# Linear attention and a gated feed-forward on one core: batch 0's first products from two terms, denominators ahead of numerators, wider dummy matmuls, and half a denominator chain moved into layer 2

## The chip, the core and the metric

The kernel runs on one core of a Trainium2 chip. The metric is the device time of one execution in microseconds (us). The engines are TensorE (PE, with its weight loads as PEld), VectorE (DVE), ScalarE (ACT), GpSimd (POOL) and SyncE (SP). The program's tiles live in SBUF, and PE writes its results to eight PSUM banks, which the kernel uses as four pairs.

## The reference

For 8 batches of 8 heads, 576 positions and head width 64, a linear attention; then a feed-forward over the 4608 positions, with 512 inputs, 1536 hidden units and 512 outputs:

```python
phi = lambda x: np.where(x > 0, x, np.exp(x) - 1.0) + 1.0
q_p, k_p = phi(q), phi(k)
kv  = np.einsum('bhsd,bhse->bhde', k_p, v)
z   = np.sum(k_p, axis=2)
num = np.einsum('bhsd,bhde->bhse', q_p, kv)
den = np.einsum('bhsd,bhd->bhs', q_p, z)[..., None] + 1e-06
x   = (num / den).transpose(0, 2, 1, 3).reshape(4608, 512)
g   = x @ w_gate
out = (g * (1 / (1 + np.exp(-g))) * (x @ w_val)) @ w_out
```

In the kernel phi(x) is max(x, 0) + min(exp(x), 1), so it has two terms that are made apart.

## The kernel before

**Layout.** The heads of a batch are handled as two halves, `lp` = 0 and 1, of four heads each. `kp` holds max(k, 0) after `mx_k`, `ek` holds exp(k) after `exp_k` (ACT) and min(exp(k), 1) after `mn_k`; `add_k` adds `ek` into `kp`, which is phi(k). `kv_corner(b, lp, t, first, last)` accumulates 36 small matmuls (64x64) of k's part `t` with v into the pair `kvp[b]`; `r_copy` copies the result to `R`. `zt` sums k's part over positions by matmuls with two columns, and `zr_copy` spreads that sum into `Zr`.

**Groups.** The positions are cut into nine groups `g` of 512. In each, layer 1 goes over 12 blocks `fb` of 128 hidden units: `l1(g, fb)` issues four matmuls with `w_gate` and four with `w_val` (128x512 each) into a pair; ACT makes `sil`, and DVE the product `hT`. Layer 2 (`lay2`, `l2_mm`) then goes over four tiles `t` of 128 positions, 12 matmuls each, and `l2_out` copies the tile out, on ACT for even `t` and on DVE for odd `t`, and stores it.

**Order.** The order is written out by hand (`manual_schedule`): each engine executes its instructions in the order of the program text, and waits only for what they need. The list `sl[fb]` holds what is issued behind `l1(g, fb)`. The pairs go round in a ring: `pair()` takes the one that was used longest ago, so a matmul that writes it waits until its last reader is through.

**The start (batch 0, lines 424 to 461).** q is transposed on PE (`qtr`), and `ph[lp]` makes phi of it: an exponential on ACT, a min on DVE, and a max-and-add on DVE. For `lp` = 1 that last operation is cut in two, `t_add_half`. `t_corners(0, Zr, lp, ps)` are the den matmuls of a half, `lnrd` their reciprocal on ACT (a logarithm and an exponential), `t_corners(0, R, lp, ps)` the num matmuls, and `x_t` multiplies num by the reciprocal into `xT` on DVE. `warm(n)` issues `n` dummy matmuls of 128 columns, whose results nobody reads; `WARM` holds their numbers. The first chunks of layer 1 (`l1_mm`, L273) are interleaved with this, and the loop over `fb` (`l1`, L289) follows.

**Batch 2 and later.** Batch 2's q is handled during group 1: `zsum` (DVE) sums phi(k), `zb` (one matmul and an ACT copy into `zbc`) spreads the sum, and the chain

```python
at: s3_prod(b, 0)          at+3: s3_prod(b, 1)
at+1: s3_reduce, s3_recip  at+4: s3_reduce, s3_recip
at+2: s3_scale, dtr        at+5: s3_scale, dtr
```

multiplies, sums, takes the reciprocal, scales `qp`, and transposes it by a DMA (`dtr`, issued by SP) into `qT`. In group 1 `at` is 6, so the last entries are behind the blocks 10 and 11. Ahead of layer 2's last tile `block(g)` issues `num` and `x_copy` for group g + 1. Between layer 1 and layer 2, POOL copies one element of `qT` into `gate` (L640), the place that the second `dtr` writes last, and only then issues the loads of batch g + 3 (L101).

Of the kernel before, what the change touches and what calls it, by code (L numbers as in the profile page):

```python
# [13 lines left out]
P = 128  # L14
# [3 lines left out]
def kernel(  # L18
# [10 lines left out]
    nc = tc.nc  # L29
# [10 lines left out]
    EPS = 1e-6  # L40
    SC = 4096.0
    NB = 3
    WARM = (36, 10, 20, 8, 6)

    sb = ctx.enter_context(tc.tile_pool(name="sb", bufs=1))
    pp = ctx.enter_context(tc.tile_pool(name="ps", bufs=1, space=bass.MemoryType.PSUM))
# [2 lines left out]
    def many(shape, dt, name, n=2):  # L49
        return [sb.tile(shape, dt, name=f"{name}_{i}") for i in range(n)]  # L50
# [4 lines left out]
    ek = many([P, 2, J, 2 * D], FP16, "ek")  # L55
    eq = many([P, HL, J * D], FP16, "eq")
    kp = many([P, 2, J, 2 * D], FP16, "kp")
# [4 lines left out]
    Zr = many([P, 2, 2, D], FP16, "Zr")  # L62
# [17 lines left out]
    ones = sb.tile([P, P], FP16, name="ones")  # L80
# [7 lines left out]
    pp4 = [[pp.tile([P, 512], FP32, name=f"pp_{2 * i + e}") for e in range(2)] for i in range(4)]  # L88
# [15 lines left out]
    def ld2(src, dst, b):  # L104
        ld(src, dst, b, 0)
        ld(src, dst, b, 1)
# [10 lines left out]
    def act(out, in_, func=AF.Copy, scale=1.0, bias=0.0):  # L117
        nc.scalar.activation(out=out, in_=in_, func=func, bias=bias, scale=scale)  # L118

    def warm(n):  # L120
        for _ in range(n):
            nc.tensor.matmul(out=pp4[2][1][:, 0:P], lhsT=ones[:, :], rhs=ones[:, :], start=True, stop=True)

    def hs(lp):
        return slice(2 * lp, 2 * lp + 2)
# [1 line left out]
    def jl(t, b, lp):  # L127
        return t[b % 2][:, lp, :, :].rearrange("p j (l d) -> p l j d", d=D)

    def lj(t, b, lp):  # L130
        return t[b % NB][:, hs(lp), :].rearrange("p l (j d) -> p l j d", d=D)
# [7 lines left out]
    def mx_k(b, lp):  # L139
        nc.vector.tensor_scalar(out=jl(kp, b, lp), in0=lj(kr, b, lp), scalar1=0.0, scalar2=None, op0=ALU.max)  # L140
# [13 lines left out]
    def add_k(b, lp):  # L154
        a = kp[b % 2][:, lp, :, :]
        nc.vector.tensor_tensor(out=a, in0=ek[b % 2][:, lp, :, :], in1=a, op=ALU.add)  # L156
# [19 lines left out]
    def kv_corner(b, lp, t, first, last):  # L176
        ps = kvp[b]
        for j in range(J):
            for l2 in range(2):
                for hh in range(2):  # L180
                    rows = slice(C * hh, C * hh + C)
                    nc.tensor.matmul(out=ps[hh][D * l2:D * l2 + D, D * lp:D * lp + D],  # L182
                                     lhsT=t[b % 2][rows, lp, j, D * l2:D * l2 + D],
                                     rhs=vr[b % NB][rows, 2 * lp + l2, D * j:D * j + D],
                                     start=(first and j == 0), stop=(last and j == J - 1))
# [6 lines left out]
    def r_copy(b, l0, l1, engs):  # L192
        for hh in range(2):
            src = kvp[b][hh][:, D * l0:D * l1].rearrange("p (l d) -> p l d", d=D)
            if engs[hh] == "A":
                act(R[b % 3][:, l0:l1, hh, :], src)
            else:
                nc.vector.tensor_copy(out=R[b % 3][:, l0:l1, hh, :], in_=src)
# [38 lines left out]
    def units(g):  # L237
        us = [(u // J, u % J) for u in range(U * g, U * g + U)]
        res = []
        for b in sorted(set(u[0] for u in us)):  # L240
            js = [j for (bb, j) in us if bb == b]
            res.append((b, js[0], js[-1] + 1, C * us.index((b, js[0]))))
        return us, res
# [146 lines left out]
    def zt(b, lp, ps, t, first, last):  # L390
        for j in range(J):
            nc.tensor.matmul(out=ps[:, 0:2], lhsT=t[b % 2][:, lp, j, :], rhs=ob[:, 0:P:C],
                             start=(first and j == 0), stop=(last and j == J - 1))
# [5 lines left out]
    def lnrd(ps, i, w0=0, w1=512):  # L399
        for l2 in range(2):  # L400
            act(lnt[2 * i + l2][:, w0:w1], ps[l2][:, w0:w1], AF.Ln, bias=epsb[:, 0:1])
            act(rd[i][:, l2, w0:w1], lnt[2 * i + l2][:, w0:w1], AF.Exp, scale=-1.0)
# [8 lines left out]
    def t_corners(g, W, lp, ps):  # L411
        for (b, j0, j1, c0) in units(g)[1]:
            corners(ps, W[b], b, lp, j0, j1, c0)

    def t_add_half(lp, ps, h):
        a = qT[0][:, lp, 4 * h:4 * h + 4, :, :].rearrange("p j h c -> p (j h c)")
        nc.vector.scalar_tensor_tensor(out=a, in0=ps[:, 256 * h:256 * h + 256].bitcast(FP16), scalar=0.0, in1=a,
                                       op0=ALU.max, op1=ALU.add)

    pq = pp4[0]  # L420
    kvp[0] = pp4[1]
    ph = [t_phi_main(0, lp, pq[lp]) for lp in range(2)]
    for l in range(2):
        nc.vector.tensor_copy(out=qr[0][:, l, :], in_=q32[:, l, :])
    warm(WARM[0])
    for lp in range(2):
        qtr(0, lp, pq[lp])
        warm(WARM[1 + lp])
        ph[lp][0]()
# [3 lines left out]
    ph[0][2]()  # L433
    mx_k(0, 0)
    zt(0, 0, pp4[3][0], kp, True, False)
    warm(WARM[3])
    mn_k(0, 0)
    zt(0, 0, pp4[3][0], ek, False, True)
    ph[1][1]()
    zr_copy(0, 0, pp4[3][0])  # L440
    warm(WARM[4])
    t_corners(0, Zr, 0, pp4[2])
    lnrd(pp4[2], 0)
    mx_k(0, 1)
    mn_k(0, 1)
    zt(0, 1, pp4[3][1], kp, True, False)
    zt(0, 1, pp4[3][1], ek, False, True)
    add_k(0, 0)
    kv_corner(0, 0, kp, True, True)
    zr_copy(0, 1, pp4[3][1])  # L450
    t_add_half(1, pq[1], 0)
    r_copy(0, 0, 1, "VV")
    t_add_half(1, pq[1], 1)
    t_corners(0, R, 0, pp4[0])
    x_t(0, 0, pp4[0], (0,))
    t_corners(0, Zr, 1, pp4[3])
    lnrd(pp4[3], 1)
    kv_corner(0, 1, kp, True, False)
    kv_corner(0, 1, ek, False, True)
    x_t(0, 0, pp4[0], (1,))  # L460
# [14 lines left out]
    def none():  # L475
        return [[] for _ in range(FB)], [[] for _ in range(4)]

    def lam(f, *a):
        return lambda: f(*a)
# [26 lines left out]
    def chain(b, at):  # L506
        return {
            at: [lam(s3_prod, b, 0)],
            at + 1: [lam(s3_reduce, b, 0), lam(s3_recip, b, 0)],
            at + 2: [lam(s3_scale, b, 0), lam(dtr, b, 0)],  # L510
            at + 3: [lam(s3_prod, b, 1)],
            at + 4: [lam(s3_reduce, b, 1), lam(s3_recip, b, 1)],
            at + 5: [lam(s3_scale, b, 1), lam(dtr, b, 1)],
        }
# [93 lines left out]
    for g in range(NG):  # L608
        b1, b2 = g + 1, g + 2
        if g == 0:  # L610
            sl = period0()
        else:
            sl, _ = none()
            if g == 1:
                sl[1] = [lam(zsum, b1)]
                sl[4] = [lam(phi_q, b1, 0), lam(zb, b1)]
                sl[5] = [lam(phi_q, b1, 1)]
                ch = chain(b1, 6)
            elif b1 < B:
                sl[0] = [lam(phi_q, b1, 0)]  # L620
                sl[1] = [lam(phi_q, b1, 1)]
                ch = chain(b1, 2)
            else:
                ch = {}
            for f, v_ in ch.items():
                sl[min(f, FB - 1)] += v_
        for fb in range(FB):
            if g == 0:
                if fb < 2:
                    continue  # L630
                if fb == 4:
                    ld2(k, kr, 2)
                    ld2(q, qr, 2)
                    ld2(v, vr, 2)
            l1(g, fb)
            for f in sl[fb]:
                f()
        if g + 3 < B:
            if g > 0:
                nc.gpsimd.tensor_copy(out=gate[:, :], in_=qT[b1 % 2][:, 1, J - 1, 1, C - 1:C])  # L640
            ld2(k, kr, g + 3)
            ld2(v, vr, g + 3)
            if g > 0:
                ld2(q, qr, g + 3)
        if g == 0:
            layer2_0()
            ld2(q, qr, 3)
        else:
            for t in range(4):
                if t == 0 and b2 < B:  # L650
                    exp_k(b2, 0)
                    exp_k(b2, 1)
                    exp_q(b2, 0)
                    exp_q(b2, 1)
                    phi_k(b2, 0)
                    phi_k(b2, 1)
                    zsum(b2)
                if g == 1 and t == 2:
                    kv_all(b1)
                    r_copy(b1, 0, 2, "AA")  # L660
                if t == 3:
                    block(g)
                if g == NG - 1 and t == 3:
                    l2_open(g, t)
                    o = None
                    for (n0, n1) in ((0, 256), (256, 512)):
                        for fb in range(FB):
                            l2_mm(g, t, fb, n0, n1)
                        o = l2_out(g, t, "V" if n0 == 0 else "A", n0, n1, o)
                    continue  # L670
                lay2(g, t)
                l2_out(g, t, "AV"[t % 2])
            if b2 < B:
                zb(b2)
# [30 lines left out]
```

## Time and profile before

| | |
|---|---|
| median of 5 runs | 320.27 us (319.1 to 320.51) |
| profiled execution | 320.51 us; its span in the trace 318.6 us |
| granted TensorE clock, mean | 0.987 |
| PE busy | 310.7 us, 98% of the span |
| PEld busy | 148.1 us, 46% |
| DVE busy | 203.6 us, 64% |
| ACT busy | 150.8 us, 47% |
| POOL busy | 48.6 us, 15% |
| moved by DMA | 32.52 MB in 41163 packets |

Times in the profile are counted from the span's start. The time of an execution is longer than the span, by 1.9 us here. "Granted clock" is the share of the full TensorE clock. In a timeline row the first number is the start, the second the duration; what ended the engine's idle time stands in brackets. Matmuls are pipelined: the spacing of their starts is their cost, and the duration printed includes a tail that the next one overlaps.

### The profile page before, as it was taken

To read this page: it belongs to the slowest core of one execution; us is meant where nothing else is said; L and a number is where in the kernel's file an instruction comes from. 1 tells how busy PE (TensorE), PEld (TensorE's weight loads), DVE (VectorE), ACT (ScalarE), POOL (GpSimd) and SP (SyncE) were. 2 spreads that over 40 slices of the span, in tenths; PEclk is the share of its full clock that TensorE was granted. 3 is DMA by queue.
4 is the path that set the end of the run, shared out by engine and by line. 5 is a ranking of instruction groups with operands and counts; after the bars stand their busy time and mean duration, and the time that the engine had idled before them with its cause. 6 is when DMAs were issued, how large, how long until landed. Compare 5 with 4: busy or idle time off the path is not lost.

```text
span 318.6 us, 5702 instructions
## 1 busy us (share of the span) xinstructions
PE 310.7 (98%) x2276; PEld 148.1 (46%) x2276; DVE 203.6 (64%) x356; ACT 150.8 (47%) x227; POOL 48.6 (15%) x73
## 2 busy tenths in 40 slices
PE   7899999999999999999999999999999999999994
PEld 6644444444544454444444454445444444444443
DVE  2844885999849874987499739973992343234420
ACT  2764859736543474347533753385331333133311
POOL 7665343000400050005000600000000000000000
PEclk9879999999999999999999999999999999999999
DMA  8999999911694389037903790215023400140014
GB/s 155 197 198 199 206 206 207 248 46 37 113 209 75 74 116 237 5 74 110 246 3 66 106 239 21 50 29 130 0 39 70 99 3 1 33 101 0 0 33 101
DMA packets 41163, 32.52 MB, mean 102 GB/s; under 512 B 16432, under 2 KB 36400, under 8 KB 41136
## 3 DMA queue, kind: packets, MB, share of 16 engines
q0 software_dynamic: 20736, 18.58, 38.0%
q1 hardware_dynamic: 20320, 13.51, 17.3%
q8 instruction: 18, 0.29, 0.4%
q10 hardware_dynamic: 80, 0.07, 0.1%
q14 instruction: 9, 0.07, 0.1%
HBM read 37.75 MB, written 9.44 MB: 148 GB/s over the span
## 4 chain that ended last, share of the span: by engine, by line
PE 87%; ACT 5%; DVE 4%; DMA 2%; issue 1%; POOLq 0%
PE pp L289 54%; PE pp L296 27%; DMA qr<-in_q_dram 2%; PE pp L251 2%; PE pp L182 2%; PE pp L273 2%; ACT lnt L118 1%; DVE hT L282 1%; ACT ek L118 1%; ACT rd L118 1%; ACT eq L118 1%; PE pp L367 1%; ACT L118 0%; DVE den L217 0%; DVE qp L226 0%
## 5 line engine op out<-in xcount | busy, mean ns | idle before, releaser
L118 ACT ACTIVATE sil<-pp 128x512 f16<-128x512 f32 x108 | 63.3, 597 | 103.1 <-PE pp L289 90.6
L289 PE MATMUL pp<-xT,wg 128*128 128x512 f16 x424 | 108.8, 379 | 0.0
L289 PE MATMUL pp<-xT,wv 128*128 128x512 f16 x424 | 108.8, 379 | 0.0
L282 DVE SCALAR_TENSOR_TENSOR hT<-pp,sil 128x512 f16<-128x512 f32 x108 | 72.0, 680 | 48.1 <-PE pp L289 34.5
L296 PE MATMUL pp<-wo,hT 128*128 128x512 f16 (+1 forms) x444 | 97.7, 374 | 0.9 <-DVE osb L319 0.5
L296 PEld LDWEIGHTS <-hT 128*128 128x128 f16 x444 | 42.0, 98 | 49.4 <-issue 1.9
L289 PEld LDWEIGHTS <-wv 128*128 128x128 f16 x424 | 41.5, 98 | 50.0
L289 PEld LDWEIGHTS <-wg 128*128 128x128 f16 x424 | 41.5, 98 | 49.3
L319 DVE TENSOR_SCALAR osb<-pp 128x512 f32<-128x512 f32 (+1 forms) x20 | 13.2, 674 | 31.4 <-PE pp L296 31.4
L118 ACT ACTIVATE osb<-pp 128x512 f32<-128x512 f32 (+1 forms) x17 | 9.8, 579 | 34.9 <-PE pp L296 34.9
L118 ACT ACT_TABLE_LOAD x14 | 18.0, 1283 | 2.8 <-PE pp L289 2.6
L640 POOL COPY gate<-qT 128x1 f16<-128x1 f16 x4 | 1.5, 379 | 107.4 <-DVE hT L282 77.1
L118 ACT ACTIVATE ek<-kr 128x1152 f16<-128x1152 f16 x16 | 17.8, 1154 | 0.2
L226 DVE TENSOR_TENSOR qp<-qp,rden 128x1152 f16<-128x1152 f16 x12 | 16.1, 1346 | 0.0
L217 DVE TENSOR_REDUCE den<-prod 128x18 f32<-128x1152 f16 x12 | 16.1, 1342 | 0.0
L268 DVE TENSOR_SCALAR xT<-pp 128x512 f16<-128x512 f32 (+1 forms) x14 | 8.7, 667 | 7.4 <-PE pp L251 7.3
L118 ACT ACTIVATE eq<-qr 128x1152 f16<-128x1152 f16 x12 | 13.2, 1148 | 0.0
L101 POOL DMA_DIRECT2D vr<-in_v_dram x16 | 11.8, 736 | 5.2 <-DMA wo<-in_moe_w_out_dram 1.8
L101 POOL DMA_DIRECT2D kr<-in_k_dram x16 | 11.6, 724 | 5.6 <-DMA wo<-in_moe_w_out_dram 1.9
L101 POOL DMA_DIRECT2D qr<-in_q_dram x15 | 10.8, 723 | 6.5 <-DMA qr<-in_q_dram 1.9
L156 DVE TENSOR_TENSOR kp<-ek,kp 128x1152 f16<-128x1152 f16 x15 | 11.4, 758 | 0.5
L144 DVE TENSOR_SCALAR ek<-ek 128x1152 f16<-128x1152 f16 x16 | 7.3, 456 | 6.0 <-ACT ek L118 6.0
(67 smaller groups left out, 182.5 us busy)
## 6 DMA issues: line engine op xcount, KB each, us to landing
out_dram<-osb SPq DMA_DIRECT2D x70, 128.0 KB, 5.0
kr<-in_k_dram POOLq DMA_DIRECT2D x16, 288.0 KB, 6.9
vr<-in_v_dram POOLq DMA_DIRECT2D x16, 288.0 KB, 10.2
qr<-in_q_dram POOLq DMA_DIRECT2D x15, 288.0 KB, 12.2
wo<-in_moe_w_out_dram POOLq DMA_DIRECT2D x3, 512.0 KB, 13.5
wg<-in_moe_w_gate_dram POOLq DMA_DIRECT2D x5, 256.0 KB, 9.3
wv<-in_moe_w_val_dram POOLq DMA_DIRECT2D x5, 256.0 KB, 9.8
q<-in_q_dram SPq DMA_DIRECT2D x1, 576.0 KB, 3.7
```

Source lines behind the costliest of these rows:

```text
L101: nc.gpsimd.dma_start(out=dst[b % NB][:, 2 * lp:2 * lp + 2, :], in_=src[b].rearrange("(l a) (c j) d -> (a c) l (j d)", a=2, j=J)[:, 2 * lp ...
L118: nc.scalar.activation(out=out, in_=in_, func=func, bias=bias, scale=scale)
L144: nc.vector.tensor_scalar(out=a, in0=a, scalar1=1.0, scalar2=None, op0=ALU.min)
L156: nc.vector.tensor_tensor(out=a, in0=ek[b % 2][:, lp, :, :], in1=a, op=ALU.add)
L182: nc.tensor.matmul(out=ps[hh][D * l2:D * l2 + D, D * lp:D * lp + D], lhsT=t[b % 2][rows, lp, j, D * l2:D * l2 + D], rhs=vr[b % NB][rows, 2 ...
L217: nc.vector.tensor_reduce(out=den[:, c, :], in_=prod[:, :, :].rearrange("p j (l d) -> p (j l) d", d=D), axis=AX.X, op=ALU.add)
L226: nc.vector.tensor_tensor(out=qv, in0=qv, in1=rden[:, c, :].unsqueeze(2).to_broadcast([P, 2 * J, D]), op=ALU.mult)
L268: nc.vector.tensor_scalar(out=dst, in0=ps[l2][:, c0:], scalar1=1.0 / SC, scalar2=None, op0=ALU.mult)
L282: nc.vector.scalar_tensor_tensor(out=hT[g % 2][:, fb, :], in0=ps[1][:, :], scalar=SC, in1=s[:, :], op0=ALU.mult, op1=ALU.mult)
L289: nc.tensor.matmul(out=ps[h][:, :], lhsT=w[:, c, P * fb:P * fb + P], rhs=xT[g % 2][:, c, :], start=(c == 0), stop=(c == 3))
L296: nc.tensor.matmul(out=l2p[(g, t)][:, n0:n1], lhsT=hT[g % 2][:, fb, P * t:P * t + P], rhs=wo[:, fb, n0:n1], start=(fb == 0), stop=(fb == F ...
L319: nc.vector.tensor_scalar(out=o[:, n0:n1], in0=ps[:, n0:n1], scalar1=1.0 / SC, scalar2=None, op0=ALU.mult)
```

## The change

In the start:

- batch 0's first kv corner (`lp` = 0) is accumulated from `kp` and `ek` apart, 72 matmuls, and `add_k(0, 0)` is gone;
- the min of q's second half is ahead of `mn_k(0, 0)`, `mx_k(0, 1)` ahead of `zr_copy(0, 0)`, and the max-and-add of q's second half is one operation of 1024 columns behind `mn_k(0, 1)`;
- `zt` of `ek` for `lp` = 1 stands behind the kv corner, and the den matmuls of `lp` = 1, with `lnrd`, stand ahead of the num matmuls of `lp` = 0;
- the dummies: 34, 14 and 16 of 128 columns, then 7, 3, 5 and 4 of 256 columns. The last two sets are new and write a bank of `pp4[1]`.

In group 1: `zb` is behind block 5, not 4; the chain's entries 10 and 11 (the second half's `s3_reduce`, `s3_recip`, `s3_scale` and `dtr`) are taken out of the blocks and issued at the beginning of layer 2. In the program that is behind the gate copy and the loads of batch 4.

```diff
-    WARM = (36, 10, 20, 8, 6)
+    WARM = (34, 14, 16, 7, 3, 5, 4)
...
-    def warm(n):
+    def warm(n, w=1, ps=None):
         for _ in range(n):
-            nc.tensor.matmul(out=pp4[2][1][:, 0:P], lhsT=ones[:, :], rhs=ones[:, :], start=True, stop=True)
+            nc.tensor.matmul(out=(ps or pp4[2][1])[:, 256:256 + P * w], lhsT=ones[:, :],
+                             rhs=ones[:, :].unsqueeze(1).to_broadcast([P, w, P]), start=True, stop=True)
...
     zt(0, 0, pp4[3][0], kp, True, False)
-    warm(WARM[3])
+    warm(WARM[3], 2)
+    ph[1][1]()
     mn_k(0, 0)
     zt(0, 0, pp4[3][0], ek, False, True)
-    ph[1][1]()
+    mx_k(0, 1)
     zr_copy(0, 0, pp4[3][0])
-    warm(WARM[4])
+    warm(WARM[4], 2)
     t_corners(0, Zr, 0, pp4[2])
     lnrd(pp4[2], 0)
-    mx_k(0, 1)
+    zt(0, 1, pp4[3][1], kp, True, False)
     mn_k(0, 1)
-    zt(0, 1, pp4[3][1], kp, True, False)
+    ph[1][2]()
+    kv_corner(0, 0, kp, True, False)
+    kv_corner(0, 0, ek, False, True)
     zt(0, 1, pp4[3][1], ek, False, True)
-    add_k(0, 0)
-    kv_corner(0, 0, kp, True, True)
+    r_copy(0, 0, 1, "VV")
     zr_copy(0, 1, pp4[3][1])
-    t_add_half(1, pq[1], 0)
-    r_copy(0, 0, 1, "VV")
-    t_add_half(1, pq[1], 1)
+    warm(WARM[5], 2, pp4[1][1])
+    t_corners(0, Zr, 1, pp4[3])
+    lnrd(pp4[3], 1)
     t_corners(0, R, 0, pp4[0])
     x_t(0, 0, pp4[0], (0,))
-    t_corners(0, Zr, 1, pp4[3])
-    lnrd(pp4[3], 1)
+    warm(WARM[6], 2, pp4[1][1])
     kv_corner(0, 1, kp, True, False)
...
             if g == 1:
                 sl[1] = [lam(zsum, b1)]
-                sl[4] = [lam(phi_q, b1, 0), lam(zb, b1)]
-                sl[5] = [lam(phi_q, b1, 1)]
+                sl[4] = [lam(phi_q, b1, 0)]
+                sl[5] = [lam(phi_q, b1, 1), lam(zb, b1)]
                 ch = chain(b1, 6)
+                late = ch.pop(10) + ch.pop(11)
...
         else:
+            for f in late:
+                f()
             for t in range(4):
```

## The prediction

> **What bounds the kernel now.** I read the page first, for the engines and the chain that ended last.
>
> ```profile
> span 318.6 us, 5702 instructions
> PE 310.7 (98%) x2276; PEld 148.1 (46%) x2276; DVE 203.6 (64%) x356; ACT 150.8 (47%) x227; POOL 48.6 (15%) x73
> ...
> PE 87%; ACT 5%; DVE 4%; DMA 2%; issue 1%; POOLq 0%
> ```
>
> PE is the bound: 98% busy, and 87% of the chain. Time can come only from PE's gaps and from matmuls that run slowly. Between 90 us and the last 6 us PE's matmuls follow each other without a gap, so the start and batches 1 and 2 are all there is to win. Next, the stretches of the start (columns: length, busy time of PE, PEld, DVE, ACT, POOL, granted clock, DMA share, GB/s):
>
> ```profile
> 3.28:6.69 3.41, 3.20 (x35) 2.64 (x34) 1.06 (x3) 0.05 (x1) 3.41 (x6) 1.00 1.04 162
> 6.69:10.11 3.42, 2.71 (x54) 2.28 (x53) 2.02 (x3) 2.51 (x3) 1.92 (x3) 1.00 1.19 196
> 10.11:13.52 3.41, 2.67 (x69) 1.91 (x69) 2.69 (x8) 2.77 (x4) 2.10 (x4) 1.00 1.30 196
> 13.52:16.93 3.41, 3.10 (x116) 2.18 (x108) 2.75 (x6) 2.60 (x5) 2.79 (x5) 0.50 1.43 194
> 16.93:20.35 3.42, 3.42 (x16) 1.00 (x12) 1.16 (x4) 2.65 (x4) 1.99 (x3) 0.50 1.45 198
> ```
>
> The granted clock is 0.50 from 13.52 to 20.35 and 1.00 after. (It has no record before 6.69, where the column says 1.00; but 128-column dummies start every 0.107 us before that mark and every 0.055 after it, so the clock rose there.) PE's timeline there shows the price: in 16.93 to 20.35 a 128x512 matmul starts every 0.43 us, afterwards every 0.216 us.
>
> ```profile
> 16.98 0.61 PE L273 MATMUL pp<-xT,wg 128*128 128x512 f16 x1
> 17.39 0.63 PE L273 MATMUL pp<-xT,wv 128*128 128x512 f16 x1
> 17.81 0.63 PE L273 MATMUL pp<-xT,wg 128*128 128x512 f16 x1
> ```
>
> Last, batch 2's den chain. PE's stall at zb, from its timeline, and the one at the last hT block, from the waits:
>
> ```profile
> 62.61 1.03 PE L289 MATMUL pp<-xT,wv 128*128 128x512 f16 x4
> 63.90 0.28 PE L209 MATMUL pp<-zs,ob 128*128 128x256 f16 x1 [0.26 <-DVE zs L205]
> 64.02 1.03 PE L289 MATMUL pp<-xT,wg 128*128 128x512 f16 x4
> ```
>
> ```profile
> PE pp L296 <- DVE hT L282: 0.3, 1, 0.3
> ```
>
> The stretch from 52.0 to 85.7, and what DVE and POOL do at its end:
>
> ```profile
> 52.00:85.70 33.70, 33.02 (x247) 14.63 (x244) 33.10 (x61) 21.31 (x32) 2.68 (x5) 1.00 0.59 119
> ```
>
> ```profile
> 85.01 0.68 DVE L319 TENSOR_SCALAR osb<-pp 128x512 f32<-128x512 f32 x1
> ```
>
> ```profile
> 83.63 0.40 POOL L640 COPY gate<-qT 128x1 f16<-128x1 f16 x1 [30.29 <-DMA qT<-qp]
> ```
>
> DVE is busy 33.10 of 33.70 us: back to back, while PE has small holes. That decides the second half of the change.
>
> **The start, step by step.** The marks are times of the profiled execution; before, the first layer-1 matmul of L289 starts at 22.44.
>
> The exponentials of k (ACT, the second ends at 11.89) and the first den are not moved: zr_copy still waits for mn_k(0,0), which waits for the exponential that ends at 10.65, so the first den stays at 11.97. The min of q's second half moves into DVE's idle time ahead of 10.68: free. add_k(0,0), 0.76 us of DVE, goes; 36 more 64x64 matmuls come (the 36 of before took 0.62 with their tail, so some 0.42 of issue). The two t_add_half (0.68 each) become one 1.23 us operation, which now lies in front of the R copies: it runs 12.29 to 13.52. The first kv corner starts when v has landed (12.13) and zt(0,1) is issued, 12.6, and its second term ends near 13.7. So the R copies are at 13.8 to 14.15 (before 14.03 to 14.38), zr_copy(0,1) ends at 14.35 (before 13.52). Five wide dummies wait for the second R copy: 14.2 to 14.75. Den of the last heads runs at 14.75 (before 15.04), the first num right behind it, ending at 15.4. xT's first half is then at 15.4 to 16.1 against 15.18 to 15.87: the reorder itself costs 0.2 us here, and gains nothing by itself, since rd of the last heads (18.33 before, about 17.8 now) is needed only at 18.4.
>
> What moves the end is the clock. With it held at 1.00, and durations of warm rows of this trace: four dummies to 15.62 (v's second half landed at 14.92); 72 kv matmuls 0.87 instead of 1.51; four L273 at 0.216 = 0.86, to 17.38, instead of 1.82; num of the last heads 0.22 instead of 0.58; next four L273 0.86 instead of 1.33, to 18.46; then xT's second half is late by 0.13 (num ends at 17.8, DVE 17.84 to 18.53 and to 19.14); eight L273 take 1.72. L289 starts at 20.31 instead of 22.44, 2.13 earlier; by terms 0.15 (kv begins later) + 0.13 - 0.64 - 0.96 - 0.36 - 0.47. The lighter first dummies (34 for 36, and 14 + 16 for 10 + 20) lie ahead of waits for q, for its DMA and for kp, and cost nothing.
>
> Does the rest follow 2.1 us earlier? DMA is saturated until 66 us and does not move. Landings, from the trace's completion events, against first uses less 2.1: weights of blocks 8 and 9 at 28.5 and 29.8 against 30.7; w_out's second third 39.5 against 42; q of batch 1, second half, 40.95 against 41.0. So it follows, with nothing to spare: past 2.1 us a further gain would wait for that q.
>
> **Will the clock hold?** From the matmuls' widths, their part of the array and their rates I work out how much of the array's time each stretch fills with columns: 0.77 in 3.28 to 6.69 (the clock then rose), 0.57 in 6.69 to 10.11 (it stayed), 0.32 in 10.11 to 13.52 (it fell), 0.61 in 13.52 to 16.93 (it stayed low), 0.92 in 16.93 to 20.35 (it rose). After the change the third stretch holds ten dummies of 0.107, den 0.22 and both kv terms, 0.47 (72 of 64 columns on a quarter of the array, 0.027 each): 1.75 of 3.41, or 0.51. That lies between the 0.57 that kept it and the 0.32 that dropped it, nearer to the first. Were the boundaries elsewhere, the poorest stretch (10.9 to 14.3) would hold 0.33. The five runs lie 1.4 us apart, so boundaries may well move. I take it as held in most executions.
>
> [...]
>
> **zb one block later, and half the den chain in layer 2.** In place, each removes a PE stall: zb 64.02 - 63.48 less its own 0.11, so 0.43; hT's last block 78.99 - 78.48, so 0.51. Together PE runs 0.94 ahead. But num(2,1) in block(1) writes the pair that the t = 1 output copy (L319) has to empty, and that copy ends at 85.70, after everything in DVE's gap-free queue; the matmul behind it started at 85.75 while its neighbours had started at 85.51, so PE already waits 0.24 there. The change only reorders DVE: reduce, reciprocal and scale come behind hT instead of around it, and scale loses an overlap: after a dependent small operation the next starts 0.034 after the end, else 0.083 before it. scale starts near 79.02 instead of 78.85. So the 0.94 comes back at num(2,1) as wait, and 0.17 on top. Bounds: -1.1 if DVE were not the limit, +0.3; I take +0.17.
>
> The moved calls stand behind the gate copy, too. Gate reads the place that the second transpose writes; now it no longer waits for that transpose (83.49) but for DVE's write near 45, and POOL's six loads of batch 4 (84.14 to 88.4) are issued from some 52 us on, in the wake of batch 3's, at 1.43 us each. Alone they end near 75, used first at 111.5. Cost: nothing, if they are through before the second transpose (issued at 80.26, 78.3 now).
>
> [...] Rows here: POOL's load issues took 0.72 both beside DVE's work and without it.
>
> **The sum.** Profiled execution 320.51 (span 318.6, 1.9 around it): 320.51 - 2.13 + 0.17 = 318.55. The median of the runs is 0.24 lower, so 318.3.
>
> **Rivals.** (1) The clock falls at 13.5 all the same. Then a wide dummy costs 0.213: five end at 15.27, den and num at 16.13, four more at 16.98. That stretch fills 0.80, over the 0.77 that raised the clock, so it is up at 16.93; kv ends 17.85, the first L273 18.7, num and the next 19.8, and L289 starts at 21.6, 0.8 earlier: 320.27 - 0.84 + 0.17 = 319.6. For it: 0.51 is untested.
>
> (2) Slower: the clock falls, and rises one boundary later, at 20.35. kv then takes 1.51 to 18.5, four L273 1.71 to 20.2, and the rest runs to 23.2, 0.75 later than before: 320.27 + 0.75 + 0.17 = 321.2. The wide dummies are the price: nine of them, 1.92 us in PE's way. It decides if a stretch of 0.80 does not raise the clock; 0.61 did not, 0.77 did.
>
> (3) The ungated loads meet batch 2's second transpose. The store issued at 86.93, among loads, landed 8.3 us later; the one of 82.19, without, 3.3. With 5.0 more the transpose lands at 86.5 instead of 81.5 while num(2,1) takes it at 83.8: 2.7 late, 321.0. It needs loads still moving at 79: at 2.48 us each, as at 88 to 100.4 beside stores, they would end at 81; at 1.43, at 75. The first block's stores are gone by 66, so 75.
>
> (4) DVE does not hold num(2,1): the den part gains 1.1 instead, 317.0. Against it stands DVE's gap-free row.
>
> **Numbers.** Clock held 0.66 (318.3; own range 317.8 to 318.9), the rivals in order 0.17, 0.07, 0.05 and 0.05. 0.3%, about what a measurement of this kernel can tell from no change, is 0.96 us. Faster: nearly all of the held case (0.64), rival 4, and the better part of rival 1's spread (0.05): 0.74. Slower: rival 2 and half of rival 3, 0.09. Same: the rest, 0.17. The range 317.7 to 319.9 takes in the held case and rival 1.
>
> **What would show it.** Right: granted clock 1.00 from 6.7 on, L289 from 20.3, zb and hT without PE waits, a PE wait of over 1 us ahead of num(2,1) near 83 us, gate near 52. Wrong: 0.50 anywhere after 13 us; PE not waiting at num(2,1); transposes landing later than num needs them.

## The result, and the profile after

| | before | after |
|---|---|---|
| median | 319.68 us (318.18 to 321.25, 63 runs) | 318.59 us (317.87 to 321.06, 37 runs) |
| profiled execution | 320.51 us | 318.75 us |
| its mean granted clock | 0.987 | 0.999 |

The ratio is 0.997, with a 95% interval of 0.9961 to 0.998: the changed kernel is faster, by 1.09 us or 0.34% by the medians and 0.30% by the ratio. That is only just at the 0.3% that the prediction set as the bound, and the interval (0.2% to 0.39%) reaches to either side of it. The forecast time was 318.3 us; the gain forecast against the 320.27 us of before's first five runs was 1.97 us.

I read the profile after in the order of the prediction. First the page: the engines, and the chain that ended last.

```profile
span 317.0 us, 5777 instructions
PE 308.9 (97%) x2315; PEld 147.6 (47%) x2315; DVE 203.6 (64%) x354; ACT 150.8 (48%) x227; POOL 48.7 (15%) x73
...
PE 89%; DVE 6%; DMA 2%; issue 1%; ACT 1%; DVEq 0%; POOLq 0%
```

PE still is the bound, busy for 1.8 us less. DVE's share of the chain rises from 4% to 6%; the last fence of this section shows where.

The start comes next, in the same stretches as before (columns: length, busy time and count of PE, PEld, DVE, ACT, POOL, granted clock, DMA share, GB/s).

```profile
6.69:10.11 3.42, 2.17 (x46) 1.73 (x44) 2.40 (x4) 1.95 (x3) 1.91 (x4) 1.00 1.19 193
10.11:13.52 3.41, 3.17 (x115) 2.25 (x113) 2.70 (x6) 2.77 (x4) 2.22 (x4) 1.00 1.32 199
13.52:16.93 3.41, 3.26 (x101) 2.02 (x101) 2.18 (x8) 3.35 (x6) 2.78 (x5) 1.00 1.43 195
16.93:20.35 3.42, 3.42 (x19) 1.31 (x18) 1.29 (x2) 2.39 (x4) 2.09 (x3) 1.00 1.44 198
```

The two stretches that were granted 0.50 are at 1.00. PE's timeline shows what that makes of the first chunks of layer 1.

```profile
16.84 0.38 PE L274 MATMUL pp<-xT,wg 128*128 128x512 f16 x1
17.06 0.38 PE L274 MATMUL pp<-xT,wv 128*128 128x512 f16 x1
...
20.35 0.59 PE L290 MATMUL pp<-xT,wg 128*128 128x512 f16 x2
```

These matmuls (L273 before, L274 now) start 0.22 us apart where they had been 0.42 apart, and layer 1's loop starts at 20.35 instead of 22.44.

In batch 2's den chain both PE stalls are gone. The zb matmul (now L210) starts without a wait:

```profile
62.24 1.03 PE L290 MATMUL pp<-xT,wv 128*128 128x512 f16 x4
63.11 0.27 PE L210 MATMUL pp<-zs,ob 128*128 128x256 f16 x1
63.22 1.03 PE L290 MATMUL pp<-xT,wg 128*128 128x512 f16 x4
```

In PE's waits the row for hT is no longer there, and one for num(2,1) has come:

```profile
PE pp L252 <- DVE osb L320: 1.1, 1, 1.1
```

The chain that ends there, in order of time, is DVE's queue with nothing but 0.02 to 0.15 us of issue in between: scale, six operations of batch 3's k, the four of its `zsum`, the t = 1 output copy (L320), and only then PE's second bank of num(2,1).

```profile
77.06 1.36 DVE qp L227
78.42 0.37 DVE kp L141
...
83.24 0.69 DVE osb L320
83.93 0.04 issue
83.97 0.22 PE pp L252
```

Followed along PE's milestones, after less before in the two profiled executions, the time goes like this (the rows with "behind" take the first matmul of layer 1 or 2 that follows, the same one in both):

| PE's milestone | after less before, us |
|---|---|
| first matmul of the loop of layer 1 | -2.09 |
| behind zb | -2.53 |
| behind the last hT of group 1 | -3.05 |
| behind num(2,1) | -1.79 |
| last matmul | -1.68 |

The last row has lost 0.11 against the one above it: a hole of some 0.1 us among the kv matmuls of group 3, for which I found no cause.

### The profile page after: what moved, and what is told of

Same layout as the page of the kernel before. It is cut to its first block, busy times and chain, and to the rows that moved or that the text cites. A ratio compares the mean times of both kernels' runs of the same rounds, so it can differ in the third digit from the quotient of the medians.

```text
span 317.0 us, 5777 instructions
## 1 busy us (share of the span) xinstructions
PE 308.9 (97%) x2315; PEld 147.6 (47%) x2315; DVE 203.6 (64%) x354; ACT 150.8 (48%) x227; POOL 48.7 (15%) x73
## 4 chain that ended last, share of the span: by engine, by line
PE 89%; DVE 6%; DMA 2%; issue 1%; ACT 1%; DVEq 0%; POOLq 0%
PE pp L290 56%; PE pp L297 27%; DMA qr<-in_q_dram 2%; PE pp L252 2%; PE pp L183 2%; PE pp L274 1%; DVE hT L283 1%; DVE den L218 1%; DVE qp L227 1%; DVE ek L145 1%; PE pp L368 1%; DVE kp L157 0%; PE pp L122 0%; DVE qT L382 0%; DVE osb L320 0%
## 5 line engine op out<-in xcount | busy, mean ns | idle before, releaser
L320 DVE TENSOR_SCALAR osb<-pp 128x512 f32<-128x512 f32 (+1 forms) x20 | 13.2, 674 | 31.6 <-PE pp L297 27.1
L101 POOL DMA_DIRECT2D qr<-in_q_dram x15 | 10.9, 728 | 9.4 <-DMA vr<-in_v_dram 3.4
L157 DVE TENSOR_TENSOR kp<-ek,kp 128x1152 f16<-128x1152 f16 x14 | 10.6, 759 | 0.5
```

The lines of the kernel that those rows point to most:

```text
L101: nc.gpsimd.dma_start(out=dst[b % NB][:, 2 * lp:2 * lp + 2, :], in_=src[b].rearrange("(l a) (c j) d -> (a c) l (j d)", a=2, j=J)[:, 2 * lp ...
L320: nc.vector.tensor_scalar(out=o[:, n0:n1], in0=ps[:, n0:n1], scalar1=1.0 / SC, scalar2=None, op0=ALU.mult)
```

## The experiments

All were timed in five rounds beside runs of the kernel before on the same chip. The first four shared 29 runs of before (median 319.65 us), e5 to e8 shared 11 on a second chip (319.46), e9 and e10 shared 18 on a third (319.67). On which chip the 37 runs of the result ran is not on record, so differences of a few tenths between the sets, or against the changed kernel, are weak. Edits are against the changed kernel unless the text says otherwise.

### The two halves apart

**e1: the changed start alone,** group 1 as before.

```diff
-                sl[4] = [lam(phi_q, b1, 0)]
-                sl[5] = [lam(phi_q, b1, 1), lam(zb, b1)]
+                sl[4] = [lam(phi_q, b1, 0), lam(zb, b1)]
+                sl[5] = [lam(phi_q, b1, 1)]
...
-                late = ch.pop(10) + ch.pop(11)
```

> The changed start alone; group 1 is as before. Theory (the gain is the start's clock; the den part only moves PE's wait and adds 0.3): layer 1's block 2 starts at 20.3 as with the whole change, PE waits again for zs and for the last hT, num(2,1) runs at 85.75 - 2.09 = 83.66, and the time is 0.3 us below the whole change. Rival (the den part earns part of the gain): 0.9 us above the whole change.

Measured: 318.08 us (317.7 to 319.08), ratio 0.9957 (0.994 to 0.9973). That is 0.5 us below the whole change. The mean granted clock was 0.999 or more in all 12 runs. The start alone is worth 1.57 us at the median, not 2.13. Its profiled execution, the longest of the 12, also shows the floor that the prediction named: it was 1.82 ahead of before until PE waited for batch 1's second half of q, which landed late, at 41.94, and 1.31 ahead after it. That load was also issued late, at 28.93 against 27.55 in the changed kernel's trace; both took 13.0 to 13.1 us to land.

**e2: the den part alone,** the start as before; the chain's last entries are still behind the gate copy.

> zb one block later and half the den chain in layer 2 alone; the start is as before. Theory: the two PE stalls (0.43 and 0.51) go, the wait at num(2,1) grows from 0.24 to about 1.2 to 1.5, the time is 0.2 to 0.3 us above before; loads of batch 4 go out near 55 and land by 77 with no effect. Rival (den part earns): 0.9 us below before.

Measured: 319.98 us (318.66 to 320.66), ratio 1.0006 (0.9988 to 1.0024): no difference by its interval; by medians 0.33 us longer. The clock fell in the profiled execution, as in before, and the mean granted clock of the 12 runs lies between 0.987 and 0.995. Against before's runs of like clock on this chip, the seven at 0.987 to 0.989 have a median of 320.30 (before 320.29) and the five at 0.993 to 0.995 one of 319.76 (before 319.28). In the trace PE gains 0.43 at zb and 0.51 at hT, and loses 1.29 at num(2,1), 0.35 in all. Two rows of PE's waits lie at that last place:

```profile
PE pp L251 <- DMA qT<-qp: 0.5, 1, 0.5
...
PE pp L251 <- DVE osb L319: 0.4, 1, 0.4
```

The second transpose lands at 84.5 here, later than num(2,1) wants it, but the t = 1 copy (L319 in this kernel) is later still: PE's last piece of num(2,1) starts at 85.29, behind the copy. The transpose was issued at 79.90 and took 4.60 to land; in before and in the changed kernel it took 3.23. The ungated loads are not the reason, as rival 3 had it: the last of them landed at 75.52, before the transpose was issued. So a late transpose occurs, from a cause that no run shows, and even here it is not what ends last.

### What num(2,1) waits for

**e3: the t = 1 copy of group 1 on ACT.** This takes L320 out of DVE's queue at the one place where PE waits for it.

```diff
-                l2_out(g, t, "AV"[t % 2])
+                l2_out(g, t, "A" if g == 1 and t == 1 else "AV"[t % 2])
```

> The whole change, and in group 1 the output copy of tile t = 1 is on ACT instead of DVE, so that num(2,1) no longer waits for DVE's queue. Theory (DVE's queue holds num(2,1) by 1.1 to 1.4): the wait is gone, 1.1 to 1.3 us below the whole change, about 317.4. Rival (something else holds num(2,1), or ACT becomes as late): the time of the whole change, with the wait put down to another engine.

Measured: 316.69 us (316.35 to 317.23), ratio 0.991 (0.9883 to 0.9937). PE's timeline has no wait at num(2,1) any more:

```profile
79.64 2.54 PE L297 MATMUL pp<-wo,hT 128*128 128x512 f16 x11
82.11 0.52 PE L252 MATMUL pp<-qT,R 64*64 64x384 f16 x8
```

PE keeps what it won at zb and at hT: -2.33, -2.78, -3.29, and -3.58 behind num(2,1), where before's own 0.24 wait has gone too. The edit of one line is worth 1.9 us here, more than the whole change and more than the 1.1 to 1.3 that I expected. In the traces 1.55 of the 1.90 lies at num(2,1); 0.24 is there from the start on, and 0.11 is the hole of group 3, and those two are not the copy's doing. Before had shown the place: its copy ended at 85.70, and the matmul that it held started at 85.75.

**e6: the chain's last entries ahead of the gate copy,** so that batch 4's loads are gated by the second transpose again. DVE's order is that of the changed kernel.

```diff
+        if g > 0:
+            for f in late:
+                f()
...
-            for f in late:
-                f()
```

> The whole change, with the moved half of the den chain issued ahead of the gate copy instead of behind it: the loads of batch 4 go out near 82 again, as before. If POOL's load issues beside DVE's gap-free stretch cost something (the whole change's trace shows one DVE operation of 0.61 instead of 0.45 there): num(2,1) is 0.1 to 0.2 earlier, the time 0.1 to 0.2 below the whole change. If not, the time of the whole change.

Measured: 318.32 us (318.05 to 318.55), ratio 0.9954 (0.9936 to 0.9972). It is 2.49 ahead when group 1 begins (2.54 at the loop of layer 1) and 2.34 behind num(2,1). So the den part, gated, costs 0.15: the term for DVE's order, which the prediction had worked out as 0.17, and little else. Ungated, the profiled execution of the changed kernel paid 0.30 (2.09 to 1.79). The 0.15 between them is in one DVE operation:

```profile
63.46 0.61 DVE L149 TENSOR_SCALAR qr<-qr 128x1152 f16<-128x1152 f16 x1
63.99 0.44 DVE L153 TENSOR_SCALAR eq<-eq 128x1152 f16<-128x1152 f16 x1
```

Its neighbour of the same shape takes 0.44, and in e6 the same operation takes 0.45, 0.16 less. The traces of e2 and e4, ungated too, agree: each has one such operation there, 0.18 longer, and pays 0.35 and 0.34. POOL's row of the changed kernel for that moment:

```profile
63.10 0.72 POOL L101 DMA_DIRECT2D qr<-in_q_dram  x1 [1.95 <-DMA vr<-in_v_dram]
```

It is the last of the six ungated loads. In e6 no load is issued then: there they are issued from 81.8 on. The median of e6 is 0.27 below the changed kernel's, on the side that the traces show.

### What holds the clock

**e4: the new order and the two terms, with dummies of 128 columns** and without the last two sets.

```diff
-    WARM = (34, 14, 16, 7, 3, 5, 4)
+    WARM = (34, 14, 16, 8, 6, 0, 0)
...
-    warm(WARM[3], 2)
+    warm(WARM[3])
...
-    warm(WARM[4], 2)
+    warm(WARM[4])
```

> The whole change, with the dummies of before in the disputed stretch: 8 and 6 of 128 columns, and none in the two new places. Theory (the dummies hold the clock): the granted clock falls to 0.50 near 13 to 14 and comes back one or two boundaries later; block 2 starts 0.5 to 1.9 us later than 20.3, the time is 0.6 to 1.5 us above the whole change. Rival (the order and the two-term product earn it): within 0.3 us of the whole change, or below it, since 1.4 us of PE's dummies are gone.

Measured: 318.33 us (317.86 to 319.71), ratio 0.9962 (0.9943 to 0.9981). The mean granted clock was 0.998 or more in 8 of 12 runs (median 317.99), 0.993 to 0.995 in three (318.82 to 319.32), and 0.989 in one (319.71). So the order and the two terms, with the changed narrow dummies at the start (14 and 16 for 10 and 20), hold the clock in two thirds of the executions without any wide dummy; I had expected it to fall. Where it holds, the start is shorter, since nine dummies are out of PE's way: layer 1's loop begins 3.02 earlier than before. Then q is late:

```profile
PE pp L376 <- DMA qr<-in_q_dram: 0.7, 1, 0.7
```

q's second half lands at 41.14 and PE is 2.11 ahead from there on. This is the floor of "past 2.1 us a further gain would wait for that q".

**e5: the dummies alone,** before's order, its one-term product and its group 1. The edit is against before; the dummies that were new stand at the nearest places of before's order.

```diff
-    WARM = (36, 10, 20, 8, 6)
+    WARM = (34, 14, 16, 7, 3, 5, 4)
...
-    warm(WARM[3])
+    warm(WARM[3], 2)
...
-    warm(WARM[4])
+    warm(WARM[4], 2)
...
+    warm(WARM[6], 2, pp4[1][1])
     kv_corner(0, 0, kp, True, True)
...
     r_copy(0, 0, 1, "VV")
+    warm(WARM[5], 2, pp4[1][1])
```

> The order and the one-term product of before; only the dummies are those of the change (34, 14, 16 of 128 columns, 7 and 3 of 256, and 4 and 5 of 256 ahead of the first kv corner and ahead of the first num). Group 1 as before. If dummies alone hold the clock: mean granted clock 0.997 or more in most executions, about 318.3, as much below before as the changed start alone. If the order and the two-term product are what fills PE: the clock still falls in many executions, about 319 or above.

Measured: 317.89 us (317.67 to 318.41), ratio 0.9943 (0.9925 to 0.9962), the mean granted clock 0.997 or more in all six. The dummies alone give all that e1 gives. The reorder and the two terms bring nothing beyond that which these runs could tell: e1's ratio is 0.9957, and the intervals overlap. The floor of q shows here too: 2.59 ahead at the loop of layer 1, and 2.22 behind a wait for that load, which landed at 41.03.

### What the floors are worth

**e7: copy on ACT, narrow dummies, and q earlier.** e3 with e4's dummies, and POOL issues the load of q's second half ahead of w_out's second third.

```diff
-    ld_w2(4, 8)
     ld(q, qr, 1, 1)
+    ld_w2(4, 8)
```

> The whole change with three edits: tile t = 1 of group 1 is copied out on ACT, the dummies are 8 and 6 of 128 columns with none in the two new places, and q of batch 1's second half is loaded ahead of w_out's second third. If the landing of q is what takes back the start's gain beyond 2.1 us: layer 2's second transposes of q no longer wait for that load, and where the clock holds the time is some 0.7 to 0.9 below the variant with the copy on ACT, near 316.0; where it falls, near 317.5. If q's landing is not what holds it: no lower than 316.5.

Measured: 316.43 us (315.96 to 317.54), ratio 0.9898 (0.9876 to 0.992). The clock held in four runs (315.96 to 316.78) and the mean was 0.994 to 0.995 in two (316.73 and 317.54). The 2.96 of its start is kept, no wait for q; behind num(2,1) it is 4.27 ahead of before. The four held runs have a median of 316.04, where 316.0 was expected for q as the floor.

**e8: the same with the change's wide dummies.**

> The whole change, with tile t = 1 of group 1 copied out on ACT and q's second half of batch 1 loaded ahead of w_out's second third; the change's own dummies. The start reaches layer 1's block 2 some 0.9 later than without the wide dummies, so q's landing hardly binds: the time of the variant with the copy on ACT, 316.7, or 0.1 to 0.3 below it. If wide dummies cost nothing, the same as the variant without them.

Measured: 316.52 us (316.19 to 317.0), ratio 0.9898 (0.9877 to 0.9918), the mean granted clock 0.997 or more in all six. It starts 0.54 later than e7, not 0.9, and the medians are 0.09 apart: what the wide dummies cost on PE they seem to bring back in the executions in which e7's clock fell, as far as six runs of each can tell. These two have the lowest ratios; both beat before by 1.0%, and the changed kernel besides.

**e9: everything that had paid so far:** e5's start, zb behind block 5, e6's place for the chain's end, e3's copy on ACT, e7's place for q.

> What the runs point to: the order and one-term product of before with the change's dummies, zb one block later, the moved half of the den chain ahead of the gate copy, tile t = 1 of group 1 copied out on ACT, q's second half of batch 1 loaded ahead of w_out's second third. If the parts add up: below the dummies alone (317.9) by the two PE stalls, 0.94, by before's own wait of 0.24 at num(2,1), and by up to 0.3 of q's landing: 316.4 to 316.7; no PE wait ahead of num(2,1). If DVE takes back what PE gains at another place, 317 or above.

Measured: 316.96 us (316.74 to 317.29), ratio 0.9924 (0.9896 to 0.9952): above the 316.4 to 316.7 that I expected, and not better than e7 and e8. PE's timeline has one new wait, for the second transpose:

```profile
81.62 0.36 PE L252 MATMUL pp<-qT,R 64*64 64x384 f16 x4
82.25 0.36 PE L252 MATMUL pp<-qT,R 64*64 64x384 f16 x4 [0.28 <-DMA qT<-qp]
```

The transpose, issued at 77.68, took 4.53 to land, at 82.21. In the ten traces other than this one and e2's it took 3.21 to 3.23; so it would have landed at 80.9, ahead of its use. It is thus not PE's lead of 3.7 that makes it late. Batch 4's loads are not the reason either, for they are issued from 82.86 on; no run shows what is. 0.28 goes there, and another 0.15 at 115.5, in a hole among kv matmuls like that of group 3 in the changed kernel.

**e10: e9 with before's zb and den chain.**

> The same, but with zb and the den chain where they were before. If moving them pays once DVE's queue no longer holds num(2,1): PE waits again at zb (0.4) and at the last hT (0.5), and the time is 0.9 above the other. If lifting the copy alone earned it: the same time as the other.

Measured: 317.4 us (317.17 to 318.12), ratio 0.994 (0.9922 to 0.9958). The waits at zb and hT are back (0.3 each in PE's waits), and it is 0.44 us behind e9. So with the copy out of DVE's queue the den part gains 0.44 by the medians, half of its 0.94, and 0.33 in the two traces: there e9 loses 0.46 against e10 at num(2,1), at the wait for the transpose, and 0.15 in the hole. In the changed kernel, with the copy on DVE, the traces show the den part as a loss.

## Why the prediction was right or wrong

**Right: the place of the gain.** L289 was to start at 20.31 and started at 20.35. The clock held, as I gave it 0.66: 35 of the 38 runs of the changed kernel, the profiled one among them, have a mean of 0.997 or more. The three others (0.994 to 0.995) are at 320.06, 320.17 and 321.06. The marks of the start came within 0.3 us of the working. Rivals 1 and 2, in which the clock falls, do not describe the profiled execution.

**Right: the den part gains nothing.** The stalls went (0.43 and 0.51), and came back at num(2,1), as a wait for the t = 1 copy of 1.05 us at 83.97; the forecast was a wait of over 1 us near 83. Rival 4 is out: DVE does hold num(2,1), and e3 shows that it does so through the t = 1 copy. Rival 3 is out too: the loads' last landing is at 75.01, where 75 was worked out, and the second transpose, issued at 78.58, landed at 81.81, before its use at 82.41.

**Right: the reorder by itself.** "Gains nothing by itself" is what e5 against e1 shows. e4 adds what I had not credited: without wide dummies it holds the clock in two executions of three.

**The floor of q** was right as well: e1, e4 and e5 met it, e7 lifted it.

**Wrong: the base that the term of 2.13 was taken from.** The sum went 320.51 - 2.13 + 0.17, "the median of the runs is 0.24 lower". The 2.13 is true of an execution that spends two stretches of 3.4 us at half rate, as the profiled one of before did, and I took the runs to be like it. They are not. The 58 runs of before beside the experiments fall into three sets by their mean granted clock:

| mean granted clock | half-rate stretches by that mean | runs | median, us |
|---|---|---|---|
| 0.987 to 0.989 | two | 31 | 320.19 |
| 0.992 to 0.995 | one | 23 | 319.28 |
| 1.000 | none | 4 | 317.99 |

(The number of stretches is worked out: one costs 0.5 x 3.41 / 318 = 0.005 of the mean. The clock also falls at the program's end, 1.32 us ahead of the span's end in before's trace, 0.48 in the changed kernel's and up to 1.65 in the others, which takes up to 0.003 more.) Two stretches take 2.2 us, which is the 2.13; but nearly half of the executions have one or none, so that removing all of them is worth less at the median: 1.57 in e1. That is 0.56 of the 0.88 by which the gain fell short of its 1.97. The two medians say the same: 0.59 of the 0.88 is the base (320.27 over five runs, 319.68 over 63), and only 0.29 the changed kernel (318.59 for 318.3). Against the four runs of before whose clock held, the changed kernel, held too (median 318.57), is not faster at all, so far as four runs on two chips can say: by them its whole gain is the clock.

**Wrong in size: the den part, 0.17.** The medians of e1 and of the whole change are 0.5 apart, though the intervals of their ratios overlap and they may not have run on one chip. The trace shows 0.30 for the den part, 0.15 for DVE's order (e6) and 0.15 for the operation that was stretched beside the ungated loads. "Cost: nothing" was the wrong step there: I looked at where the loads land, and not at what DVE was doing while POOL issued them. I had also read before's rows as 0.72 for a load's issue beside DVE's work and without it; that holds at 84 to 88 us, but the same trace has issues of 0.77 to 0.82 at 114, 145 to 147 and 177 to 179. The remaining 0.2 is open: it may be no difference at all, or q's landing, which took between 0 and 0.9 from the lead in these traces.

**The boundaries.** That a stretch of 3.41 us decides the clock of the next was my assumption. The changes in before's trace do lie whole multiples of that length apart (last section); what decides at such a mark no run shows. I had worked out a fill of 0.51 for the third stretch with the boundaries of before's trace, and 0.33 for the poorest place, and wrote that boundaries "may well move". They move: the mark at which the clock rises lies anywhere between 3.94 (e1) and 6.69 (before) in the twelve profiled executions, at 5.87 in the changed kernel's. With the same working of the fill (widths, part of the array, rates), on each execution's own boundaries, the poorest stretch between the rise and 17 us is:

| kernel | poorest fill | clock after it |
|---|---|---|
| before | 0.32 | 0.50 |
| e2 (before's start) | 0.30 | 0.50 |
| e7 | 0.40 | 1.00 |
| e5 | 0.41 | 1.00 |
| e1 | 0.42 | 1.00 |
| after, e4, e9 | 0.43 | 1.00 |
| e3 | 0.47 | 1.00 |
| e10 | 0.50 | 1.00 |
| e6, e8 | 0.52 | 1.00 |

The fill separates the two that fell from the ten that held, with the edge between 0.32 and 0.40; that the clock goes by the fill itself is not shown. It would also say why e7 and e4 lose the clock in some executions: in their traces a stretch begun elsewhere would hold as little as 0.27 and 0.30, but at least 0.34 in the eight others that held, and 0.40 in the changed kernel's. That is argued; the runs without a trace show only their mean, and the changed kernel too lost the clock in three of 38. At before's marks its third stretch holds 0.52, where I had 0.51, and 10.9 to 14.3 holds 0.43, where I had 0.33. The stretch of e2 that followed the fall was filled to 0.49 and did not raise the clock, as 0.61 had not in before.

Busy time can be set beside that. The falls came after stretches in which PE was busy for 2.67 us (before) and 2.65 us (e2) of 3.41:

```profile
8.87:12.28 3.41, 2.65 (x52) 1.81 (x50) 2.53 (x8) 2.77 (x4) 1.59 (x3) 1.00 1.28 193
12.28:15.70 3.42, 2.82 (x80) 1.88 (x82) 3.23 (x8) 2.53 (x5) 2.83 (x4) 0.50 1.36 196
```

while e5's clock stayed after a stretch with the same busy time:

```profile
7.51:10.92 3.41, 2.67 (x53) 2.31 (x48) 2.60 (x6) 2.65 (x3) 1.70 (x3) 1.00 1.20 197
10.92:14.33 3.41, 2.80 (x69) 1.87 (x68) 3.33 (x9) 3.12 (x5) 1.50 (x3) 1.00 1.32 195
```

Busy time does not separate the two; the fill of those first rows does, 0.30 against 0.55.

## What to carry to other kernels

Before a gain is counted from one profiled execution, sort the runs by their mean granted clock and see how many are like it: a gain that removes a disturbance is worth only the share of executions that have it. Where PE waits at the end of a gap-free queue of another engine, taking stalls out ahead of that queue gives nothing; taking one operation out of the queue gave more here than all the rest. And an experiment that lifts one floor should name the next with its landing or ending time: here the start's gain met q, and the den part's the output copy. A wait seen in one trace may be that execution's own, as the late transposes of e2 and e9 may be.

## What the runs showed of the hardware

In the profiled execution of before the clock rises at 6.69, falls at 13.52, rises at 20.35 and falls at 317.31 us: 6.83, 6.83 and 296.96 us lie between, which are 2, 2 and 87 times 3.41. In that of the changed kernel it rises at 5.87 and falls at 316.48, 310.61 us or 91 times 3.41 later. The place against the program differs from one execution to the next: the first rise lies 2.75 us earlier in e1 (3.94) than in before (6.69). By the mean clocks of its runs (0.987 to 0.989, 0.992 to 0.995, 1.000) the same kernel, before, so has executions with two, one and no half-rate stretch at its start.

A max or min of 16-bit data in SBUF (`TENSOR_SCALAR` of 128x1152, 0.45 us alone) on DVE and a load's issue on POOL (0.72 us alone) do not always keep their times where they meet. Which of them takes longer goes, in the traces of before and of the changed kernel behind 24 us, with how far the DVE operation starts behind the issue. At 0.29 to 0.45 us it is DVE's operation, in all four such rows: 0.72 and 0.71 us at 0.29 (changed kernel, 143.40 and 144.83), 0.61 at 0.36 (changed kernel, 63.46, above) and 0.53 at 0.45 (before, 31.95). e2 and e4 have 0.63 at 0.34 (DVE at 58.52, POOL at 58.18; 56.05 and 55.71). At 0.16 to 0.23 us DVE kept its 0.45, and POOL's issue took 0.77 to 0.83 instead of 0.72, in all nine. From 0.56 us on both kept their times. The additions of two such operands (`TENSOR_TENSOR`, 0.76 us) took 0.76 in all 17 rows that overlap an issue. So either can be the one that takes longer, by 0.08 to 0.27 us for DVE and 0.05 to 0.11 for POOL; the prediction had looked at POOL's issues alone. The issue's row begins first in both kinds, so its beginning is not what settles it; what does, no run shows.
